# The product of w_out with phi: phi held in four column groups, the turned w_out streamed, the parts added by a second product

## The chip, the core and the metric

The kernel runs on one core of a Trainium2 chip. The metric is the device time of one execution in microseconds; the number that counts is the median of several. Before the change it is 575.36 us (three runs, 575.34 to 577.53).

## What is computed

Causal attention with a decay, then a dense feed-forward layer, then a soft mixture of experts; every result leaves in float32.

```python
x = attention(q, k, v, f)                  # 4 x 8 heads, 576 positions, head size 64 -> 2304 x 512
h = x @ w_in                               # 512 -> 2048
g = h * (1.0 / (1.0 + np.exp(-1.702 * h)))
x = g @ w_out                              # 2048 -> 512
logits = x @ phi                           # 512 -> 32 slots
d = softmax(logits, axis=0); slot_input = d.T @ x
slot_out[e] = relu(slot_input[e] @ w1[e]) @ w2[e]    # 8 experts, 4 slots each
out = softmax(logits, axis=1) @ slot_out
```

The kernel never forms the logits from `x`. It forms `wphi = w_out @ phi` (2048 x 32) once and computes the logits as `g @ wphi`. The change concerns how `wphi` is made.

## The kernel before

Attention goes through 20 rows (four batches, each with four blocks of 128 positions and one of 64). The feed-forward layer goes through nine chunks of 256 tokens, each in eight units (`moe_steps`, L765): twelve matmuls into one PSUM tile `hp` (L775 to L777), a tanh on ScalarE (L788), a product on VectorE (L789). A finished unit is later turned by `turn` (L731): four transposes (L744), a copy on ScalarE (L751), and four products with `wphi` (L753), whose stationary operand is a 128x32 slice of `wphi`, one for each of four groups of 32 output partitions. Attention work is emitted between the units, and the expert weights are loaded once attention is over, since they take its memory.

`w_out` (2048 x 512) comes in 16 slices of 128 rows. Each is loaded by SyncE's queue (L195), rebuilt as float32 from its raw words by GpSimd, ScalarE and VectorE (L208 to L216), and handed to `fold_phi` (L240). That turns the slice on TensorE (four 128x128 transposes, L243, into the PSUM tile `woT`), copies it to SBUF on ScalarE (L245), and waits for a second slice. With two slices turned, it multiplies: for each slice `n` and each quarter `kk` of the 512 columns, the turned 128x128 quarter of the slice is stationary and the 128x32 quarter of `phi_sb` moves (L252), four products adding up in PSUM to one 128x32 result. VectorE copies the two results into `wphi` (L255). There are eight such pairs. A float32 matmul shows as two instructions in the trace, so the 64 products are 128 instructions.

The 128x128 matrix `rsum` (L80, filled at L120) has a one wherever a row and a column have the same number modulo 32; a product with its first 32 columns adds four groups of 32 partitions. The kernel already uses it so in `slot_steps` (L828, and L831, which is the shape that the change uses).

The PSUM tiles `woT`, `wps`, `hp`, `gT`, `mT` and some of the slot sums share one ring of three banks (`ps_mm`, L64). The order of the instructions on each engine, and of the transfers on SyncE's queue, is made by a planner from the order of emission and from estimated costs (L1257); TensorE, ScalarE and VectorE then run their queues in that order.

Of the kernel before, what the change touches and what calls it, by code (L numbers as in the profile page):

```python
# [10 lines left out]
F32 = mybir.dt.float32  # L11
# [19 lines left out]
def attention_moe_softmoe(ctx, tc, q, k, v, f, w_in, w_out, phi, w1, w2, out):  # L31
    nc = tc.nc
# [4 lines left out]
    NS = phi.shape[1]  # L37
# [6 lines left out]
    KD = DM // 128  # L44
# [11 lines left out]
    ap_ = attn_pool.enter_context(tc.tile_pool(name="ap", bufs=1))  # L56
# [7 lines left out]
    def ps_mm(name):  # L64
        return ps.tile([128, 512], F32, tag="mm", name=name, bufs=3)
# [14 lines left out]
    rsum = const.tile([128, 4 * NS], F32, name="rsum")  # L80
    wphi = mp.tile([128, KF, NS], F32, tag="wphi", name="wphi")
    phi_sb = const.tile([128, KD, NS], F32, name="phi_sb")
# [137 lines left out]
    def more_w(to):  # L220
        while w_at[0] < min(NW, to):
            n = w_at[0]
            w_at[0] += 1
            while w_loaded[0] < min(NW, n + W_AHEAD):
                w_load(w_loaded[0])
                w_loaded[0] += 1
            w_first(n)
            if n < NI:
                split_one(n)
            else:  # L230
                WO[n - NI] = W32.pop(n)
                if w_phi:
                    fold_phi(*w_phi.pop())
                w_phi.append((n - NI,))
        if w_at[0] == NW and w_phi:
            fold_phi(*w_phi.pop())
# [3 lines left out]
    def fold_phi(ff):  # L240
        pt = ps_mm("woT")
        for kk in range(KD):
            nc.tensor.transpose(pt[:, kk * 128:(kk + 1) * 128], WO[ff][:, kk * 128:(kk + 1) * 128], ident)  # L243
        wt_ = mp.tile([128, 512], F32, tag="gt", name="woT", bufs=N_GT)
        nc.scalar.copy(out=wt_, in_=pt)  # L245
        wot.append(wt_)
        if len(wot) < 2:
            return
        wps = ps_mm("wps")[:, 0:2 * NS].rearrange("p (f s) -> p f s", s=NS)
        for n, wt_ in enumerate(wot):  # L250
            for kk in range(KD):
                nc.tensor.matmul(  # L252
                    wps[:, n], lhsT=wt_[:, kk * 128:(kk + 1) * 128], rhs=phi_sb[:, kk, :], start=(kk == 0), stop=(kk == KD - 1)
                )
        nc.vector.tensor_copy(wphi[:, ff + 1 - 2:ff + 1, :], wps)  # L255
        wot.clear()
        folded[0] = (ff + 1) // 4
# [376 lines left out]
    for pair in range(B // 2):  # L634
# [4 lines left out]
        n = rows_of[-1]  # L639
# [399 lines left out]
    if True:  # L1039
# [26 lines left out]
        n = 0  # L1066
# [10 lines left out]
        for c in range(NCH):  # L1077
            t0, t1 = goals[c], goals[c + 1]
            NSTEP = 2 * N_UNIT
            n = 0  # L1080
# [35 lines left out]
        for hf in range(2):  # L1116
            for g in range(4):
# [3 lines left out]
                    start=True, stop=True,  # L1121
# [18 lines left out]
        for hf in range(2):  # L1140
            hsb[hf] = G[NCH - 1, 1, "ab"[hf]].rearrange("p a n -> p (a n)")
            for n in range(2):
                l1 = ps_mm("l1")
                for kk in range(KD):
                    for g in range(4):
# [3 lines left out]
                            rhs=wt[1, n, e, kk], start=(kk == 0), stop=(kk == KD - 1),  # L1149
                        )  # L1150
                    load_e(4)
                if done:
                    turn(*done[-1])
                nc.scalar.activation(
                    out=hsb[hf][:, n * 512:(n + 1) * 512], in_=l1, func=AF.Relu, scale=zi[:, hf:hf + 1]
# [9 lines left out]
        for j in range(WHOLE):  # L1165
            hf, fb = divmod(j, KE)
            for p, (c0, c1) in enumerate(PARTS):
                for g in range(4):
                    nc.tensor.matmul(
                        so[p][32 * g:32 * g + 2 * SPE, :], lhsT=hz[:, fb, hf, g, :],  # L1170
                        rhs=wt[2, None, 4 * hf + g, fb][:, c0:c1], start=(j == 0), stop=False,
# [5 lines left out]
        for p, (c0, c1) in enumerate(PARTS):  # L1177
            w = c1 - c0
            nr = 2
            for fb in range(WHOLE - KE, KE):  # L1180
                for g in range(4):
                    nc.tensor.matmul(
                        so[p][32 * g:32 * g + 2 * SPE, :], lhsT=hz[:, fb, 1, g, :],
                        rhs=wt[2, p, 4 + g, fb // 2 * 2][:, fb % 2 * w:fb % 2 * w + w],
                        start=False, stop=(fb == KE - 1),
# [10 lines left out]
                out=s4[64:128], in0=p4[64:128], scalar=SS, in1=s4[64:128], op0=ALU.mult, op1=ALU.subtract  # L1196
# [13 lines left out]
            for k, blks in enumerate(groups):  # L1210
# [10 lines left out]
                if len(blk_tok[blks[0]]) == 1:  # L1221
                    tok = blk_tok[blks[0]][0][2]
                    queue.dma_start(
                        out=out[tok:tok + 128 * m, c0:c1].rearrange("(t p) n -> p t n", p=128), in_=ob
# [37 lines left out]
```

## Time and profile before

| what | value |
|---|---|
| median of three runs | 575.36 us |
| the profiled execution, its own time | 572.58 us |
| its span | 570.9 us |
| mean granted TensorE clock | 0.97 of full speed |
| PE / DVE / ACT / POOL busy | 510.8 / 353.3 / 309.6 / 69.0 us |
| stretch in which w_out is folded with phi | about 85 to 165 us |

The profile is one execution. Its time is 0.5% below the median of the runs, so a difference is worked out against 572.58 us and then carried to the median in proportion. "PE" is TensorE's matmuls, "PEld" its loads of stationary operands, which may overlap them; busy TensorE time includes a modelled tail of each instruction. The chain of waits follows the work that ended last back from the end of the execution: a piece of it is the time from one instruction to the next one on the chain, so that for instructions in a row it is their spacing and not their latency.

### The profile page before, as it was taken

To read this page: it belongs to the slowest core of one execution; us is meant where nothing else is said; L and a number is where in the kernel's file an instruction comes from. 1 tells how busy PE (TensorE), PEld (TensorE's weight loads), DVE (VectorE), ACT (ScalarE), POOL (GpSimd) and SP (SyncE) were. 2 spreads that over 40 slices of the span, in tenths; PEclk is the share of its full clock that TensorE was granted. 3 is DMA by queue.
4 is the path that set the end of the run, shared out by engine and by line. 5 is a ranking of instruction groups with operands and counts; after the bars stand their busy time and mean duration, and the time that the engine had idled before them with its cause. 6 is when DMAs were issued, how large, how long until landed. Compare 5 with 4: busy or idle time off the path is not lost.

```text
span 570.9 us, 13573 instructions
## 1 busy us (share of the span) xinstructions
PE 510.8 (89%) x5355; PEld 328.1 (57%) x5355; DVE 353.3 (62%) x934; ACT 309.6 (54%) x596; POOL 69.0 (12%) x120
## 2 busy tenths in 40 slices
PE   4476999999899989989999998988999999999991
PEld 4364877777666556655665664655566554454441
DVE  8978969476755676757685766867565323343032
ACT  5767686666765665646675565665565133312111
POOL 4766643220000000000000000000000000000000
PEclk9969799999999999999999998998999999999997
DMA  9997673978952869997648889986553189999998
GB/s 241 270 355 168 167 126 134 206 183 163 165 95 43 150 101 132 167 180 126 125 87 159 134 158 175 200 139 91 81 94 72 24 276 357 372 388 358 378 302 262
DMA packets 229823, 105.63 MB, mean 185 GB/s; under 512 B 202592, under 2 KB 211296, under 8 KB 229760
## 3 DMA queue, kind: packets, MB, share of 16 engines
q1 hardware_dynamic: 228528, 103.59, 77.9%
q10 hardware_dynamic: 1232, 1.18, 0.7%
q8 instruction: 42, 0.69, 0.5%
q14 instruction: 21, 0.17, 0.1%
HBM read 64.63 MB, written 4.72 MB: 121 GB/s over the span
## 4 chain that ended last, share of the span: by engine, by line
PE 62%; DMA 17%; DVE 9%; ACT 5%; issue 3%; SPq 2%; POOL 0%; DVEq 0%; ACTq 0%; POOLq 0%
PE hp L775 9%; PE hp L777 8%; PE hp L776 8%; DMA ph<-pn 6%; PE gT L744 5%; DMA we<-in_moe_w_dram 4%; PE p L753 4%; PE pv L607 3%; PE sp L896 3%; DMA kf<-in_k_dram 2%; PE pv L612 2%; DMA qf<-in_q_dram 2%; PE scs L536 2%; PE scs L535 2%; DVE low L213 1%
## 5 line engine op out<-in xcount | busy, mean ns | idle before, releaser
L775 PE MATMUL hp<-w,xt 128*128 128x512 f16 x288 | 111.0, 385 | 0.8 <-DVE spart L903 0.8
L776 PE MATMUL hp<-w,xt 128*128 128x512 f16 x288 | 110.7, 384 | 0.0
L777 PE MATMUL hp<-w,xt 128*128 128x512 f16 x288 | 110.6, 384 | 0.0
L562 ACT ACTIVATE pf<-scs,mx 128x512 f32<-128x512 f32 (+3 forms) x108 | 58.3, 543 | 40.7 <-DVE mx L558 30.4
L788 ACT ACTIVATE g<-hp 128x512 f32<-128x512 f32 x72 | 42.6, 592 | 53.0 <-PE hp L777 52.9
L571 DVE SCALAR_TENSOR_TENSOR pn<-pf,pn 128x512 f16<-128x512 f32 (+2 forms) x78 | 51.0, 657 | 32.1 <-ACT pn L570 31.6
L789 DVE SCALAR_TENSOR_TENSOR g<-g,hp 128x512 f32<-128x512 f32 x72 | 49.2, 683 | 34.6 <-ACT g L788 34.4
L570 ACT ACTIVATE pn<-pf 128x512 f16<-128x512 f32 (+2 forms) x78 | 46.9, 604 | 23.4 <-DMA ph<-pn 22.3
L558 DVE CUSTOM_DVE_ANT_0 scs<-scs,zmq 128x256 f32<-128x256 f32 (+3 forms) x96 | 46.9, 497 | 11.8 <-PE scs L536 6.8
L612 PE MATMUL pv<-vv,ph 128*128 128x65 f16 (+2 forms) x360 | 46.7, 198 | 3.5 <-DMA ph<-pn 3.4
L751 ACT COPY gt<-gT 128x512 f32<-128x512 f32 x71 | 40.8, 582 | 14.3 <-PE gT L744 13.5
L777 PEld LDWEIGHTS <-xt 128*128 128x128 f16 x288 | 28.5, 99 | 34.7 <-issue 2.8
L613 PE MATMUL pv<-vv,ph 128*128 128x65 f16 (+2 forms) x360 | 46.1, 196 | 0.0
L614 PE MATMUL pv<-vv,ph 128*128 128x65 f16 (+2 forms) x360 | 45.4, 194 | 0.0
L744 PE MATMUL gT<-ident,g 128*128 128x128 f32 x288 | 44.5, 278 | 1.0 <-DVE g L789 1.0
L775 PEld LDWEIGHTS <-xt 128*128 128x128 f16 x288 | 29.0, 101 | 25.7 <-issue 3.5
L612 PEld LDWEIGHTS <-ph 128*128 128x128 f16 (+2 forms) x360 | 34.5, 101 | 14.6 <-issue 5.8
L776 PEld LDWEIGHTS <-xt 128*128 128x128 f16 x288 | 28.5, 99 | 24.0 <-issue 2.3
L744 PEld LDWEIGHTS gT<-ident,g 128*128 128x128 f32 x288 | 33.3, 142 | 14.2 <-issue 5.1
L535 PE MATMUL scs<-kab,qa 128*128 128x128 f16 x240 | 35.4, 219 | 4.4 <-ACT pf L562 2.5
L613 PEld LDWEIGHTS <-ph 128*128 128x128 f16 (+2 forms) x360 | 34.9, 103 | 2.7 <-issue 0.4
L614 PEld LDWEIGHTS <-ph 128*128 128x128 f16 (+2 forms) x360 | 35.0, 103 | 0.7 <-issue 0.6
(223 smaller groups left out, 1013.4 us busy)
## 6 DMA issues: line engine op xcount, KB each, us to landing
we<-in_moe_w_dram SPq DMA_DIRECT2D x127, 256.0 KB, 5.4
raw<-in_moe_w_in_dram SPq DMA_DIRECT2D x16, 512.0 KB, 7.6
raw<-in_moe_w_out_dram SPq DMA_DIRECT2D x16, 512.0 KB, 6.0
kf<-in_k_dram SPq DMA_DIRECT2D x13, 256.0 KB, 3.7
qf<-in_q_dram SPq DMA_DIRECT2D x13, 256.0 KB, 4.4
vf<-in_v_dram SPq DMA_DIRECT2D x12, 256.0 KB, 4.5
out_dram<-ob SPq DMA_DIRECT2D x12, 256.0 KB, 3.2
ph<-pn SPq DMA_TRANSPOSE x78, 3.3
```

The source lines that it names most:

```text
L558: nc.vector.tensor_tensor_reduce(out=o, in0=o, in1=mask, scale=-SC, scalar=3.0e38 if n == 128 else DG[r][1][:, u], op0=ALU.add, op1=ALU.mi ...
L562: nc.scalar.activation(out=pf[:, hh * nb:(hh + 1) * nb], in_=o, func=AF.Exp, bias=mx[:, hh:hh + 1], scale=-1.0)
L570: nc.scalar.activation(out=pn[:, 0, 0:w], in_=pf, func=AF.Copy, scale=PB)
L571: nc.vector.scalar_tensor_tensor(out=pn[:, 1, 0:w], in0=pf, scalar=PB, in1=pn[:, 0, 0:w], op0=ALU.mult, op1=ALU.subtract)
L612: nc.tensor.matmul(o, lhsT=ph[0:rr, 0, off:off + n], rhs=vh, start=(j == 0), stop=False)
L613: nc.tensor.matmul(o, lhsT=ph[0:rr, 0, off:off + n], rhs=vl, start=False, stop=False)
L614: nc.tensor.matmul(o, lhsT=ph[0:rr, 1, off:off + n], rhs=vh, start=False, stop=(j == i))
L744: last_turn[0] = nc.tensor.transpose((pt if a < 2 else pt2)[:, a * 128:(a + 1) * 128], g[:, a * 128:(a + 1) * 128], ident)
L775: nc.tensor.matmul(hp, lhsT=xt[:, 0, kk, ts], rhs=win(0, fg, kk), start=(kk == 0), stop=False)
L776: nc.tensor.matmul(hp, lhsT=xt[:, 0, kk, ts], rhs=win(1, fg, kk), start=False, stop=False)
L777: last_hp[0] = nc.tensor.matmul(hp, lhsT=xt[:, 1, kk, ts], rhs=win(0, fg, kk), start=False, stop=(kk == KD - 1))
L789: nc.vector.scalar_tensor_tensor(out=g, in0=g, scalar=1.0, in1=hp, op0=ALU.add, op1=ALU.mult)
```

## The change

Inside `fold_phi`, the operands of the product change places. The 128x32 quarter of `phi_sb` is now stationary and the turned 128x128 quarter of `w_out` moves; the quarter `kk` writes to output partitions 32·kk to 32·kk + 31 of a new PSUM tile `wq`. The four quarters are no longer added in PSUM. ScalarE copies the 128x256 tile to SBUF (`part`), and two products, with a 128x128 half of `part` stationary and `rsum[:, 0:32]` moving, add the quarters and give the same 128x64 result `wps`, which VectorE copies into `wphi` as before.

```diff
-        wps = ps_mm("wps")[:, 0:2 * NS].rearrange("p (f s) -> p f s", s=NS)
+        wq = ps_mm("wq")[:, 0:256]
         for n, wt_ in enumerate(wot):
             for kk in range(KD):
                 nc.tensor.matmul(
-                    wps[:, n], lhsT=wt_[:, kk * 128:(kk + 1) * 128], rhs=phi_sb[:, kk, :], start=(kk == 0), stop=(kk == KD - 1)
-                )
+                    wq[NS * kk:NS * (kk + 1), n * 128:(n + 1) * 128], lhsT=phi_sb[:, kk, :],
+                    rhs=wt_[:, kk * 128:(kk + 1) * 128], start=True, stop=True,
+                )
+        part = ap_.tile([128, 256], F32, tag="part", name="part")
+        nc.scalar.copy(out=part, in_=wq)
+        wps = ps_mm("wps")[:, 0:2 * NS].rearrange("p (f s) -> p f s", s=NS)
+        for n in range(2):
+            nc.tensor.matmul(
+                wps[:, n], lhsT=part[:, n * 128:(n + 1) * 128], rhs=rsum[:, 0:NS], start=True, stop=True
+            )
         nc.vector.tensor_copy(wphi[:, ff + 1 - 2:ff + 1, :], wps)
```

## Rows read from the trace of the kernel before

**Rows 1.** Windows: start:end, length; busy us (instructions) by engine; clock; DMA share; GB/s.
```profile
90.00:105.00 15.00, 15.00 (x192) 13.03 (x192) 13.06 (x28) 11.31 (x21) 5.75 (x7) 1.00 0.46 85
135.00:150.00 15.00, 13.33 (x123) 9.78 (x123) 10.88 (x39) 11.84 (x26) 0.00 (x0) 1.00 1.04 199
150.00:165.00 15.00, 13.36 (x160) 10.76 (x158) 9.47 (x27) 9.61 (x19) 0.00 (x0) 1.00 0.85 132
345.00:360.00 15.00, 13.44 (x141) 7.41 (x142) 10.22 (x39) 8.15 (x19) 0.46 (x8) 0.89 0.93 173
```

**Rows 2.** Chain of waits, 84 to 165 us: start, us, what; the matmuls of L252.
```profile
91.71 0.37 PE wps L252 x4
...
93.91 0.81 PE wps L252 x8
...
128.31 1.01 PE wps L252 x8
...
157.96 0.89 PE wps L252 x8
```

**Rows 3.** The same chain, its longest pieces that are not TensorE's.
```profile
105.39 6.11 DMA raw<-in_moe_w_out_dram
137.48 4.88 DMA kf<-in_k_dram
152.31 5.22 DMA ph<-pn
160.69 2.75 DMA ph<-pn
```

**Rows 4.** The same chain: the first and the last of nine ScalarE pieces.
```profile
111.58 0.43 ACT low L211
...
163.52 0.53 ACT pn L570
```

**Rows 5.** Waits of TensorE, 85 to 167 us: who, for whom, total us, times, longest.
```profile
PE scs L535 <- ACT pf L562: 1.6, 1, 1.6
PE gT L744 <- DVE g L789: 1.0, 1, 1.0
PE wps L252 <- ACT woT L245: 0.8, 1, 0.8
PE p L753 <- ACT gt L751: 0.7, 1, 0.7
PE pv L612 <- DMA ph<-pn: 0.2, 1, 0.2
```

**Rows 6.** Chain of waits elsewhere: L753 in column groups, and what follows it.
```profile
176.70 0.79 PE p L753 x24
177.49 0.16 PE scs L535
177.65 0.06 PE scs L536
...
484.50 0.57 PE p L753 x16
...
487.37 0.22 PE hp L775
...
489.96 0.44 PE gT L744 x4
490.40 0.36 PE p L753 x8
490.76 0.32 PE hp L775
...
493.45 0.36 PE p L753 x8
493.81 0.59 PE gT L744 x4
```

**Rows 7.** Chain of waits: the product of L831 with rsum's first 32 columns.
```profile
172.36 0.36 PE lg L831 x4
```

**Rows 8.** Groups by form: line engine op, shapes, count | busy us, mean ns | idle before.
```profile
L252 PE MATMUL wps<-phi_sb,woT 128*128 128x32 f32 x128 | 16.6, 272 | 0.8 <-ACT woT L245 0.8
L747 ACT COPY gt<-gT 128x256 f32<-128x256 f32 x1 | 0.4, 372 | 2.4 <-PE gT L744 2.4
L562 ACT ACTIVATE pf<-scs,mx 128x256 f32<-128x256 f32 x24 | 11.2, 473 | 6.6 <-DVE mx L558 6.3
L570 ACT ACTIVATE pn<-pf 128x512 f16<-128x512 f32 x42 | 26.3, 629 | 12.5 <-DMA ph<-pn 11.8
```

**Rows 9.** Timeline, 502 to 508 us: start, us, engine, line; one hop over ScalarE.
```profile
504.81 0.66 PE L744 MATMUL gT<-ident,g 128*128 128x128 f32 x4
505.33 0.37 ACT L747 COPY gt<-gT 128x256 f32<-128x256 f32 x1 [2.36 <-PE gT L744]
505.82 0.72 PE L753 MATMUL p<-gt,wphi 128*32 128x128 f32 x8
```

**Rows 10.** Timeline, 155 to 170 us, TensorE and VectorE: the last pair.
```profile
161.68 0.97 PE L252 MATMUL wps<-phi_sb,woT 128*128 128x32 f32 x8
165.17 0.22 DVE L255 COPY wphi<-wps 128x64 f32<-128x64 f32 x1
166.61 0.43 PE L753 MATMUL p<-gt,wphi 128*32 128x128 f32 x8
```

## The prediction

> **What bounds the kernel now.** I read the busy time in stretches first, to see who is full where `w_out` is folded with `phi`. From 90 to 105 us TensorE is busy for the whole stretch; from 135 to 165 us it is busy for 13.3 of each 15 us, while ScalarE has 9.6 to 11.8 us of work and the transfers are dense [rows 1]. So TensorE is nearly full, but not everywhere. Next come TensorE's own waits: in the 82 us from 85 to 167 they add up to 4.3 us, of which one of 0.8 us is L252 waiting for the copy L245 [rows 5]. Last comes the chain of waits. From 84 to 165 us it runs along TensorE and leaves it for four long transfers, of 6.1, 4.9, 5.2 and 2.8 us [rows 3]. The reader should see the two together: while the chain is on a transfer, TensorE is busy with other work that is just in time, so work removed from TensorE there turns into waiting, and work removed where the chain is on TensorE shortens the kernel.
>
> L252 lies on that chain in ten pieces (four stand in the rows), 64 instructions and 6.94 us in all [rows 2]. That is half of its 128 instructions [rows 8]. Eight instructions take 6.94 / 8 = 0.87 us, so L252 costs TensorE 16 x 0.87 = 13.9 us and the chain 6.94 us.
>
> **What the change removes and adds on TensorE.** Removed: 13.9 us. Added, first: per pair 16 instructions with a 128x32 float32 stationary operand and 128 float32 columns moving, in four groups of output partitions. The trace has this form: it is L753. Eight in a row take 0.36 us, 16 take 0.57, 24 take 0.79 [rows 6]. So one more costs (0.79 - 0.36) / 16 = 0.027 us, against 0.109 for one of L252, and a group has a fixed part of 0.36 - 8 x 0.027 = 0.14 us. There is a second fixed part behind it: the first `hp` matmul after a group takes 0.32 us (a next one is 0.22), the first `scs` 0.16 instead of 0.06, four transposes 0.59 (0.44 where they follow other work) [rows 6]. I charge 0.12 us. A group of eight then costs 0.48 us and one of 16 costs 0.69. Which it will be is the planner's choice. Today the half for the first slice runs while the second slice is still being copied, and L252 stands on the chain in eights [rows 2]; I expect eights. Sixteen groups of eight are 7.7 us, eight groups of sixteen 5.5 us.
>
> The fixed part is where the Trainium skill speaks against the change. In "TensorEngine Tiling (Array Packing)", section Key Properties, it says that changing the tiling mode drains TensorE, and in its section Theoretical Speedup that a dimension of up to 32 can give a factor of up to four. The trace agrees with both, 0.109 to 0.027 inside a group and about 0.26 us for entering and leaving one; by the factor of four alone the 13.9 us would become 3.5.
>
> Added, second: the two products with `rsum` per pair, four instructions. L831 is the same shape, and four of it take 0.36 us [rows 7]; with a little for their neighbours, 8 x 0.38 = 3.0 us. TensorE therefore saves 13.9 - 7.7 - 3.0 = 3.2 us with groups of eight and 13.9 - 5.5 - 3.0 = 5.4 us with groups of sixteen. On the chain lie half of the pieces: 1.6 to 2.7 us. I take the middle, 2.15 us.
>
> **What it adds elsewhere.** ScalarE gets eight copies of 128x256 float32 from PSUM. The trace has one such copy, 372 ns, and an exponential of the same size at 473 ns [rows 8]: 3.0 to 3.8 us of work, in 80 us where ScalarE is busy two thirds of the time. ScalarE holds nine pieces, 4.75 us, of the 81 us of chain, 6% [rows 4]; so 0.2 us of the copies lie on the path, and at worst all 3.8. The copy stands in ScalarE's queue ahead of exponentials and of `pn` (L570), and those are followed by the transposing transfers for attention.
>
> The new wait is on TensorE: the product with `rsum` waits for the copy, and everything queued on TensorE behind it waits too. The nearest rows are the 16 hops from L243 over L245 to L252, of which one cost TensorE 0.8 us [rows 5]. Half as many hops of that kind cost 0.4 us; a copy that is not covered costs more (below). I take 0.6 us and keep 0 and 9.6 as the ends.
>
> Nothing else moves: the loads of `w_out`, the transposes L243, the copies L245 and L255 stay as many. A pair holds a bank of the ring of three twice instead of once. No wait of TensorE in this stretch is for a bank as far as the rows show, so I cost it at nothing; the cover is the planner's freedom to put attention ahead of an `hp`, and if it is gone, the price is that of another hop. `wphi` is ready later by a copy and a product, about 0.8 us. For the last pair the matmuls start at 161.68, L255 runs at 165.17 and the first product after it at 166.61 us [rows 10]; the copy of L255 stands in VectorE's queue longer than the added steps take, so that is hidden.
>
> **Sum.** -2.15 + 0.2 + 0.6 = -1.35 us, taken as -1.4. Against the profiled execution, 572.58 us, that is 571.2; in proportion, 575.36 x 571.2 / 572.58 = 574.0 us. All later stages, the expert weights too, follow from the end of attention, so I let the shift stand to the end.
>
> **The rivals.** A measurement of this kernel can tell about 0.5% (2.9 us) from no change.
>
> 1. TensorE is the limit all along: the transfers on the chain are released by work that itself waited for TensorE, so that all 3.2 to 5.4 us arrive. For it speak the few waits of TensorE, 4.3 us in 82 [rows 5]; against it the 13.3 of 15 us between 135 and 165 [rows 1] and the four long transfers [rows 3]. About -4.2 us: 571.1 us, between 570 and 572.
>
> 2. Slower, by the uncovered hop: TensorE runs in order and stands still at each pair until ScalarE has delivered `part`. One uncovered hop shows at the end of the kernel: transposes from 504.81, four of them 0.44 us, the copy at 505.33, the next product at 505.82 [rows 9], so 505.82 - 505.25 = 0.57 us. With one instruction ahead on ScalarE, 0.63 us for L570 [rows 8], it is 1.2 us, and eight hops cost 9.6. TensorE then stands still in full, so its whole saving counts: -3.2 to -5.4 + 9.6 = +4 to +6, about 580 us. It decides from the wait per pair: 3.2 / 8 = 0.4 us eats the saving, and 0.76 us makes the kernel slower by 0.5%. Against it speaks that 15 of 16 hops of today are covered.
>
> 3. The planner sorts the queues anew, as the costs of the operations differ, and a transposing transfer or a load goes out behind its neighbour instead of ahead of it. A piece of the chain of this kind is 2.8 to 5.2 us [rows 3], so this is worth 3 to 5 us either way: 570 or 578 us. A stretch in which TensorE then idles can also lose clock: in 345 to 360 us the mean granted clock is 0.89 [rows 1], which is 22% of the 15 us, 3.3 us, at the lower level of 1.2 GHz and so some 1.6 us of work.
>
> **How the numbers follow.** The forecast has 0.46, rival 1 0.24, rival 2 0.14, rival 3 0.16 (0.06 faster, 0.04 same, 0.06 slower). The forecast reaches from -3.2 to +1 and gives 0.04 to faster and 0.42 to same; rival 1 is faster. Faster: 0.04 + 0.24 + 0.06 = 0.34. Same: 0.42 + 0.04 = 0.46. Slower: 0.14 + 0.06 = 0.20. The range runs from just below rival 1, 569.2 us, to the dearer end of rival 3 with a lost stretch of clock, 578.8 us; it leaves out most of rival 2 and the ends of rival 3.
>
> **What would show it.** The new matmuls of the product in groups of eight at about 0.36 us apiece on the chain, or sixteen at 0.57; the products with `rsum` at 0.36 us for four; eight copies of about 0.37 us on ScalarE; TensorE's busy time lower by 3 to 6 us; few waits of TensorE for `part`. The forecast is wrong if TensorE waits for ScalarE's copy at most of the pairs, if the saved time is still there at 165 us and gone at 450, or if a span of the same length shows other transfers on the chain than before.

## The result, and the profile after

The kernel with the change takes 568.77 us (median of six runs, 566.11 to 570.59) against 575.35 us for the kernel before on the same chip: a ratio of 0.9865 with a 95% interval of 0.9828 to 0.9903. The forecast was 574.0 us in a range from 569.2 to 578.8; the result lies just below it. The two medians are 6.6 us apart; by the ratio, which is used below throughout, the gain is 7.8 us (1.35% of 575.35), and by its interval 5.6 to 9.9. The forecast's 1.4 us is a quarter of the lowest of these. The profiled execution of after took 569.88 us with a span of 568.1 us. Executions more than 1.5% above the fastest of their kernel (the slow ones) are left out of all that follows, which leaves 94 of the 103 runs of before that were timed beside the experiments, and a ratio is turned into us with their median, 574.0 us.

Behind L263 the lines of after are 8 higher than those of before; the column products keep L252, the copy of the part is L257, the products with `rsum` are L260.

The windows of after that answer to [rows 1] (start:end, length; busy us and instructions of PE, PEld, DVE, ACT, POOL; clock; DMA share; GB/s):

```profile
90.00:105.00 15.00, 15.00 (x201) 11.78 (x204) 14.53 (x30) 12.33 (x23) 7.07 (x8) 1.00 0.58 124
135.00:150.00 15.00, 10.31 (x145) 6.98 (x142) 9.90 (x31) 9.23 (x19) 0.00 (x0) 1.00 1.12 174
150.00:165.00 15.00, 13.43 (x148) 9.39 (x148) 7.70 (x23) 8.58 (x18) 0.00 (x0) 0.77 0.40 74
345.00:360.00 15.00, 15.00 (x169) 8.90 (x167) 11.02 (x43) 7.89 (x20) 0.61 (x8) 1.00 0.93 170
```

In the stretch of the fold, TensorE is idle more than before (10.3 busy of 15 us instead of 13.3) and has lost clock behind it (0.77). At 345 us, where the edit touches nothing, TensorE is now full and has its whole clock, where before showed 13.4 us and 0.89. The last copy into `wphi` (L263) starts later than before's 165.17 us [rows 10]:

```profile
L263 DVE COPY wphi<-wps x8: 208/216/221, 96.4 to 170.8; 128x64 f32<-128x64 f32 x8
```

The gain is not where the edit is.

The chain of waits of after, 84 to 165 us (start, us, what; answers to [rows 2, 3, 7]):

```profile
93.28 0.36 PE wq L252 x8
...
94.57 0.56 PE wps L260 x4
...
101.29 5.24 DMA kf<-in_k_dram
...
108.34 0.45 PE wps L260 x4
...
120.11 0.63 PE wps L260 x4
...
134.82 4.99 DMA kab<-kan
...
145.19 5.01 DMA ph<-pn
...
150.22 0.52 ACT pn L578
150.75 0.27 ACT part L257
151.06 1.06 PE wps L260 x4
```

Eight column products take 0.36 us, as worked out from L753. The products with `rsum` take 0.45 to 0.63 us and not 0.36, and the one at 151.06 us takes 1.06, at a lower clock. The four lines from 145.19 us on are the hop of rival 2 in a form that the prediction did not see: the copy of the part stands on ScalarE behind a `pn`, and that waits for a transposing transfer.

TensorE's waits of after, 85 to 167 us (who, for whom, us in total, times, longest; answers to [rows 5]):

```profile
PE wps L260 <- ACT part L257: 5.5, 3, 4.6
PE scs L459 <- ACT pf L481: 1.5, 1, 1.5
PE p L761 <- ACT gt L759: 0.8, 1, 0.8
PE pv L620 <- DVE x L634: 0.3, 1, 0.3
```

and the windows around the longest of them (columns as above):

```profile
147.00:150.00 3.00, 0.00 (x0) 0.00 (x0) 2.12 (x7) 1.63 (x3) 0.00 (x0) 1.00 1.33 135
150.00:153.00 3.00, 1.94 (x9) 1.85 (x10) 2.72 (x8) 2.31 (x5) 0.00 (x0) 0.60 0.95 163
153.00:156.00 3.00, 3.00 (x9) 1.06 (x7) 0.64 (x2) 1.07 (x2) 0.00 (x0) 0.50 0.38 70
156.00:159.00 3.00, 3.00 (x27) 1.85 (x25) 0.42 (x1) 0.88 (x2) 0.00 (x0) 0.76 0.00 0
```

TensorE stands still for 4.6 us, and then works for some 7 us at the lower level of 1.2 GHz. All waits of the stretch add up to 8.1 us, against 4.3 before. So after is faster in spite of a worse fold, 5.6 us later at its end (3.8 us in the repeats: 166.8 against 163.0).

### The profile page after: what moved, and what is told of

Its sections match the earlier page's. It is cut to its first block, busy times and chain, and to the rows that moved or that the text cites. A ratio compares the mean times of both kernels' runs of the same rounds, so it can differ in the third digit from the quotient of the medians.

```text
span 568.1 us, 13632 instructions
## 1 busy us (share of the span) xinstructions
PE 508.9 (90%) x5387; PEld 319.4 (56%) x5387; DVE 352.7 (62%) x934; ACT 309.8 (55%) x604; POOL 69.4 (12%) x120
## 4 chain that ended last, share of the span: by engine, by line
PE 66%; DMA 16%; DVE 7%; ACT 5%; issue 2%; SPq 1%; POOL 0%; DVEq 0%; ACTq 0%; POOLq 0%
PE hp L783 10%; PE hp L784 9%; PE hp L785 9%; DMA ph<-pn 7%; PE gT L752 5%; DMA we<-in_moe_w_dram 5%; PE p L761 4%; PE pv L615 3%; PE sp L904 3%; PE pv L620 3%; DMA kf<-in_k_dram 2%; PE scs L543 2%; PE pv L622 2%; PE scs L544 2%; PE pv L621 2%
## 5 line engine op out<-in xcount | busy, mean ns | idle before, releaser
L752 PE MATMUL gT<-ident,g 128*128 128x128 f32 x288 | 46.1, 280 | 0.0
L620 PEld LDWEIGHTS <-ph 128*128 128x128 f16 (+2 forms) x360 | 34.2, 101 | 18.4 <-issue 10.3
L752 PEld LDWEIGHTS gT<-ident,g 128*128 128x128 f32 x288 | 33.2, 142 | 13.4 <-issue 5.7
L577 POOL MEMSET pn<- 128x128 f16 x12 | 2.5, 211 | 268.3 <-DMA ph<-pn 113.9
```

Source lines behind the costliest of these rows:

```text
L620: nc.tensor.matmul(o, lhsT=ph[0:rr, 0, off:off + n], rhs=vh, start=(j == 0), stop=False)
L752: last_turn[0] = nc.tensor.transpose((pt if a < 2 else pt2)[:, a * 128:(a + 1) * 128], g[:, a * 128:(a + 1) * 128], ident)
```

## The experiments

**The floor and the repeat.** The unchanged kernel before, and the change once more.

> The kernel before, once more, as a control: ratio 1.000 within 0.3%. Its second profile shows which of the first one's stalls and clock losses belong to the kernel (they stand at the same place) and which to one execution. The first profiled execution was 572.58 us and the timed ones about 575.35; if the 2.8 us between them are chance of one execution, this profile lies between 572 and 577 us with the same order of work on each engine.

576.4 us, a ratio of 1.0055 (1.0023 to 1.0086) for the very same program, outside the 0.3% that were expected. Differences of half a per cent are not to be read, whatever their interval.

> The changed kernel once more, beside the others of this group. As in its first comparison: 0.9865 of the kernel before. The kernel before against itself had come out at 1.0055 in the last group, so 0.982 to 0.992 would agree.

566.18 us, 0.9858 (0.9812 to 0.9903). The gain repeats.

**The terms of the sum.** First the part copied by VectorE, so that it no longer stands behind `pn`:

```diff
-        nc.scalar.copy(out=part, in_=wq)
+        nc.vector.tensor_copy(part, wq)
```

> The changed kernel with the copy of part on VectorE instead of ScalarE; all TensorE work is the same. Theory A (the kernel shortens by the TensorE time that the change saves): 568 to 570 us as the changed kernel, since TensorE has the same work; the 13 us for which TensorE waited for part move to VectorE or shrink. Theory B (the gain is the planner's new order of the queues, and another order gives another time): no relation to 568.8; anything from 566 to 577 us.

564.32 us, 0.986 (0.9826 to 0.9894). TensorE's waits of this run, 75 to 175 us, show the hop nearly gone:

```profile
PE wps L260 <- DVE part L257: 1.7, 2, 1.2
```

The 13 us of the expectation count the waits of TensorE's products (6.0 us) and of their loads (7.2 us), which are largely the same. The ratio is that of the change within its interval. The long hop costs less than these runs can tell.

Then the column products issued twice:

```diff
-                nc.tensor.matmul(
-                    wq[NS * kk:NS * (kk + 1), n * 128:(n + 1) * 128], lhsT=phi_sb[:, kk, :], ...
+                for _ in range(2):
+                    nc.tensor.matmul(
+                        wq[NS * kk:NS * (kk + 1), n * 128:(n + 1) * 128], lhsT=phi_sb[:, kk, :], ...
```

> The changed kernel with each product in the column groups issued twice (the second writes the same values): 128 more instructions, at 0.027 us apiece 3.4 us more TensorE time, and no other change. Theory A: 568.8 + 3.4 = 572.2 us. The prediction's rule, half of it: 570.5. Theory B: a new order again, anything from 566 to 577 us.

575.71 us, 1.0049 (1.0016 to 1.0082). 128 more instructions at 0.027 us are 3.5 us, and the kernel is 10.6 us slower than the change (1.0049 less 0.9865, of 574.0). Two thirds of that are not the work that was added.

And the product of before cut to one of its four quarters:

```diff
-            for kk in range(KD):
+            for kk in range(1):
```

> The kernel before with only the first of the four products of each sum (wphi is then a quarter of the sum): 96 of 128 instructions of 0.109 us leave TensorE, 10.4 us, with no new hop and no new copy. Theory A: 565 us (all 10.4 us arrive). The prediction's own rule, half of it lies on the chain: 570 us. Theory B: no clear relation to the TensorE time taken away; it may be no faster than 572.

554.8 us, 0.9691 (0.9657 to 0.9725), or 17.7 us, where three quarters of L252's 13.9 us, 10.4 us of TensorE's time, were taken out. Again the time moved by more than the work. In each of these kernels the planner had sorted the queues anew. In the traces the queues can be compared instruction by instruction. Of TensorE's 5227 instructions outside the fold's own products, 373 in e2 and 1242 in e4 stand in another order than in the change, and 1173 in e3 in another than in before.

**Work and order apart.** The order of every engine's queue was recorded from before and from after, and then forced on other work by an edge (an added dependency) from each instruction to the next:

```diff
+        for text in ORDER:
+            keys = [int(x) for x in text.split()]
+            for x, y in zip(keys, keys[1:]):
+                tc.add_manual_dep(by[y], by[x].name, ..., reason="order")
```

> The product as in the kernel before (the old operands, no part, no products with rsum), but every engine's queue in the order of the changed kernel, as recorded from its program; SyncE's queue is the same instruction by instruction. Theory A (the TensorE time saved is the gain): as the kernel before, ratio 1.00. Theory B (the new order is the gain): as the changed kernel, 0.986 to 0.99.

567.23 us, 0.9878 (0.9836 to 0.9919): the product of before in the order of after has nearly all of the gain, 7.0 us, without the change. Its trace holds the queues of after on every engine, but for the fold's own products and copies.

> The product as in the changed kernel (wps in a free part of wq's bank), but every engine's queue in the order of the kernel before; only the eight copies of part and the sixteen products with rsum are put in by the planner, and L255 is free. Theory A: as the changed kernel, 0.986 to 0.99; by my prediction's sum 0.9975; if all 3.2 to 5.4 us arrive 0.991 to 0.994. Theory B: 1.00, or above it by the hops.

571.93 us, 0.9953 (0.9919 to 0.9988): the product of after in the order of before gains 2.7 us, no more than before differed from itself in e1. Here `wps` had to share the bank of `wq`, which brings one wait of 2.5 us of its own (the waits view of this run: `wq` for VectorE's `wphi`), so that the work alone may be worth up to 5 us in the old order; in the new order it is worth 0.7 us (0.9878 less 0.9865, inside the noise).

> Only the first of the four products of each sum, as in e3 (wphi is a quarter of the sum), with every engine's queue in the order of the kernel before. It takes 10.4 us off TensorE and changes nothing else. Theory A: -10.4 us, ratio 0.982, or half of it by the rule of the chain, 0.991. Theory B, in which most of e3's 18.5 us came from the new order: 0.99 to 1.00. If it comes out near e3's 0.969, neither the order nor the plain TensorE time explains it.

564.15 us, 0.9826 (0.978 to 0.9873). In the old order, 10.0 us are gained for some 10.4 us taken off TensorE. Half of them, 5.2 us, lies outside the interval (7.3 to 12.6), and the other 7.7 us of the free quarter came from its order. That the 10.0 us are TensorE's work alone is not shown: the three stalls that the next part finds in before are gone too (no wait of TensorE between 170 and 370 us is over 1.1 us), and the mean clock is 0.967 against 0.9625.

No run forced the old order on the old work alone. But the queues of this run, and of e9, e13 and e14 below, are in the traces those of before on every engine, but for what was left out or filled in. So the edges themselves changed no order.

**What a good order has.** TensorE's waits between 170 and 370 us, of the repeat of before and then of the old work in the new order:

```profile
PE pv L612 <- DMA ph<-pn: 3.1, 1, 3.1
PE lg L828 <- DVE l L820: 2.3, 1, 2.3
PE scs L535 <- DMA qa<-qan: 1.8, 1, 1.8
```

```profile
PE p L980 <- ACT gt L978: 2.3, 4, 1.2
PE pv L839 <- DMA ph<-pn: 1.1, 2, 0.8
PE pv L839 <- DVE x L853: 1.0, 1, 1.0
```

The old work in the old order has three single stalls of 1.8 to 3.1 us, which the first profile of before shows as well (2.8, 2.3 and 1.9 us, at 207, 251 and 346.5 us); the new order has none above 1.2 there. The stalls belong to work and order together: with the new work in the old order (e7) TensorE has no wait over 1.4 us between 170 and 370 us, though that profile is of the fastest of its 12 executions. The windows behind the stalls, of the repeat of before, and then the same windows of the new order (columns as above):

```profile
204.00:207.00 3.00, 1.67 (x21) 1.48 (x21) 1.74 (x7) 1.98 (x6) 0.00 (x0) 0.50 0.47 89
207.00:210.00 3.00, 3.00 (x10) 1.27 (x10) 2.87 (x12) 1.35 (x3) 0.00 (x0) 0.50 0.00 0
...
252.00:255.00 3.00, 3.00 (x10) 2.10 (x11) 2.06 (x7) 0.20 (x1) 0.18 (x2) 0.50 0.92 176
255.00:258.00 3.00, 3.00 (x14) 1.51 (x12) 1.53 (x8) 0.45 (x3) 0.00 (x0) 0.50 1.11 242
...
351.00:354.00 3.00, 3.00 (x44) 2.66 (x44) 1.78 (x9) 1.38 (x4) 0.00 (x0) 0.50 0.95 180
```

```profile
207.00:210.00 3.00, 3.00 (x24) 1.38 (x24) 2.90 (x11) 1.08 (x4) 0.00 (x0) 1.00 1.23 111
...
252.00:255.00 3.00, 3.00 (x30) 0.96 (x28) 2.92 (x11) 2.63 (x6) 0.00 (x0) 1.00 1.12 195
255.00:258.00 3.00, 3.00 (x35) 1.80 (x28) 3.00 (x9) 2.25 (x5) 0.00 (x0) 1.00 1.04 150
```

The reader should see TensorE busy for 3.00 of 3.00 us in both, but with 10 instructions at clock 0.50 and 24 at 1.00. Busy time alone hides the loss. The same two places in the first profile of before, behind stalls of 2.8 and 2.3 us, have their whole clock:

```profile
207.00:210.00 3.00, 3.00 (x31) 1.87 (x32) 2.65 (x11) 2.53 (x6) 0.00 (x0) 1.00 0.46 87
252.00:255.00 3.00, 3.00 (x21) 1.68 (x21) 2.74 (x13) 0.74 (x4) 0.18 (x2) 1.00 0.95 195
```

That led to a theory, the theory A of the next expectations (further up the letter stood for the work): the order gains clock. A run of TensorE at 1.2 GHz follows a stall, in some executions of the old order and not in others.

To test it, products whose results the next product overwrites were put where TensorE stands still, in the old work and the old order:

```diff
+FILL = {2241: 60, 2758: 16, 4230: 24}   # ahead of which instruction, how many products
...
+            for _ in range(FILL[n]):
+                nc.tensor.matmul(out_, lhsT=ident16[:, 0:rows], rhs=rhs, start=True, stop=True)
```

> The product of before, every queue held to the order recorded from before, and in three places where TensorE stands still in every execution of that order (2.8 to 3.1 us ahead of L612 near 207 us, 2.3 us ahead of L828 near 251 us, 1.9 us ahead of L535 near 346 us) products whose results the next product overwrites: 60 of 65 columns, 16 of 256 and 24 of 128, so that TensorE is busy while it waits. Theory A (most of the 6.8 us that the new order is worth is clock that the old order loses after these stalls): the mean granted clock of the timed runs rises from 0.9615 to 0.968 to 0.973, no fall stands near 204 to 210, 252 to 258 and 350 to 357 us, and the ratio to before is 0.988 to 0.995. Rival B (the order is worth its time through who waits for whom, and the clock follows it): the ratio is 0.999 to 1.006, since the added products are at best hidden. Rival C (the falls move to the next stall): clock as before, 0.9615, ratio 0.998 to 1.005.

570.41 us, 0.9952 (0.9918 to 0.9985), mean clock 0.9717: the clock is as theory A has it, the time a hair beyond its dear end. One fall is still there, against the theory. TensorE's timeline around 250 us (start, us, engine, line, what; idle before it) and a window behind it show why:

```profile
250.49 3.57 PE L297 MATMUL lg<-ident 128*128 128x256 f16 x16 [2.67 <-DVE l L1063]
```

```profile
252.00:255.00 3.00, 3.00 (x15) 2.28 (x13) 0.00 (x0) 0.00 (x0) 0.00 (x0) 0.50 0.98 200
```

The filling at the second place waited itself, 2.67 us for VectorE's `l`, and then ran for 3.57 us at half clock. The next run puts it ahead of the last group before the stall.

> As e9_filled_stalls (the product and the order of before, overwritten products where TensorE stands still), but at the second place they stand ahead of the last scores-times-values group before the stall instead of behind the wait for VectorE's l, where they had waited too and then ran for 3.6 us at half clock. 70 products of 65 columns near 207 us, 60 of 65 columns near 248 us, 24 of 128 columns near 346 us. Theory A (the old order loses clock after its stalls, and that is what the new order gains): mean granted clock of the timed runs 0.972 to 0.977 and a ratio of 0.985 to 0.992, since the 3.4 us that the misplaced products cost are gone. Rival B (the gain of e9_filled_stalls is a shift of the order's timing, not clock): a ratio of 0.994 to 1.003 and a clock as in e9_filled_stalls or lower.

566.69 us, 0.9898 (0.9843 to 0.9952), mean clock 0.9732. Timeline and windows of this run:

```profile
203.15 2.29 PE L297 MATMUL pv<-ident 128*128 128x65 f16 x70
...
206.35 0.20 PE L855 MATMUL pv<-vv,ph 128*128 128x65 f16 x1 [0.91 <-DMA ph<-pn]
...
247.44 2.09 PE L297 MATMUL pv<-ident 128*64 128x65 f16 x60
```

```profile
207.00:210.00 3.00, 3.00 (x20) 1.54 (x18) 2.56 (x11) 1.86 (x4) 0.00 (x0) 1.00 0.34 64
252.00:255.00 3.00, 3.00 (x26) 2.05 (x25) 2.38 (x14) 1.81 (x6) 0.00 (x0) 1.00 1.09 213
```

2.3, 2.1 and 1.5 us of useless work, 5.9 us in all, make the kernel of before 5.9 us faster and give it the clock of the new order. The data for which TensorE waited come no sooner for it: ahead of 206.35 us, 2.29 us of filling and 0.91 of waiting are 3.2 us, where the stall had 2.8 and 3.1.

> The control: as many overwritten products, 33, 30 and 24 of 128 columns, some 5 us in all, in the same order of before, but each placed some us behind a stall, where TensorE is busy anyway. Theory A: they fill nothing, so the mean granted clock stays at 0.959 to 0.964 and the ratio is 1.004 to 1.010. Rival B (more activity anywhere, or a shift of timing, helps): clock 0.967 or more, ratio below 1.000.

571.31 us, 0.9965 (0.9933 to 0.9996), clock 0.9692. This went against what theory A expected of it, and clock and ratio are both those of rival B: as much added work, where TensorE is busy, neither slowed the kernel nor left the clock alone. The trace shows that the control was not a clean one:

```profile
205.45 0.20 PE L855 MATMUL pv<-vv,ph 128*128 128x65 f16 x1 [2.84 <-DMA ph<-pn]
216.78 2.01 PE L297 MATMUL scs<-ident 128*128 128x128 f16 x33
```

```profile
207.00:210.00 3.00, 3.00 (x9) 1.12 (x8) 2.44 (x12) 1.35 (x3) 0.00 (x0) 0.54 0.24 49
249.00:252.00 3.00, 3.00 (x37) 2.44 (x37) 2.05 (x6) 1.22 (x2) 0.50 (x10) 1.00 0.86 169
252.00:255.00 3.00, 3.00 (x21) 1.69 (x20) 2.32 (x13) 1.20 (x5) 0.14 (x2) 1.00 0.93 179
348.00:351.00 3.00, 2.90 (x54) 2.33 (x47) 2.79 (x14) 2.18 (x6) 0.00 (x0) 0.78 0.94 179
```

The first stall has its 2.84 us and its fall, as in before. But TensorE comes to the second place some 2 us later than it would have, the data are there, and that stall is gone: added work upstream may do as well as work in the stall. At the third place, too, the 1.8 us have become two waits of 0.58 and 0.41 us, and yet the clock falls behind them (0.78). So e14 does not tell filling from shifting, and a fall does not need one long stall. It does show that 5.3 us of added work (2.0, 1.8 and 1.5 us) can cost nothing.

**Are new orders good ones?** Two edits that add and remove no work. Here the second slice of a pair goes first:

```diff
-        for n, wt_ in enumerate(wot):
+        for n, wt_ in reversed(list(enumerate(wot))):
```

> The product of before, with the same 128 instructions of L252, emitted for the second slice of a pair ahead of the first; nothing else is edited and the planner sorts the queues from it anew. No work is added or removed. Theory (the planner's new order decides by several us whatever the edit is): a ratio outside 0.995 to 1.005, either sign, most likely 0.985 to 0.993 or 1.007 to 1.015; clock and time move together. Rival (new orders scatter little, and the gain of the order of after is special to its work): 0.997 to 1.003.

567.45 us, 0.9888 (0.9849 to 0.9926): 6.4 us for an edit that does no work. Of TensorE's 5227 instructions outside the fold's products, 1209 stand in another order than in before.

Here the first slice is multiplied as soon as it is turned:

```diff
+        if n == 0:
+            w_ps.append(ps_mm("wps")[:, 0:2 * NS].rearrange("p (f s) -> p f s", s=NS))
+        wot.append(wt_)
+        wps = w_ps[-1]
+        for kk in range(KD):
+            nc.tensor.matmul(wps[:, n], lhsT=wt_[:, kk * 128:(kk + 1) * 128], rhs=phi_sb[:, kk, :], ...)
+        if len(wot) < 2:
+            return
```

> The product of before, with the same 128 instructions of L252, but those of the first slice of a pair are emitted as soon as that slice is turned, and its bank of the ring is taken there; nothing else is edited, and the planner sorts the queues anew. No work is added or removed. Theory (the planner's order decides): a ratio outside 0.995 to 1.005, either sign. Rival (orders scatter little): 0.997 to 1.003. If this and the run with the second slice first both stay within 0.5% of before, the order of after is a rare find; if one is faster by over 1%, the 6.8 us can be had without any change of work.

577.19 us, 1.006 (1.0025 to 1.0095), which can't be told from the 1.0055 of before itself. The same two edits on the kernel after:

> The change, with the column products of the second slice of a pair emitted ahead of those of the first; no work is added or removed, and the planner sorts the queues anew. It answers e10_second_slice_first, which is the same edit of the kernel before. Theory (work of the change 2 to 3 us, the rest is which order the planner happens to make): a ratio to before anywhere from 0.980 to 1.002, and not the same as that of the change, 0.9865, by more than 0.3%. Rival (the operations of the change lead the planner to a good order, whatever the emission): 0.984 to 0.988.

565.43 us, 0.9857 (0.9811 to 0.9902): no other than the change, as the rival has it. But it is hardly another order: 57 of the 5227 instructions stand otherwise than in the change. What does differ is the hop, 0.5 us in all between 75 and 175 us instead of 6.0, and that brought nothing that can be told.

> The change, with the column products of the first slice of a pair emitted as soon as it is turned, and its bank taken there; the same edit as e11_first_slice_early, on the change. Theory: 0.980 to 1.002, as that edit was worth +0.6% on the kernel before and the work of the change is worth 0.4%: most likely near 1.000. Rival (the operations lead to a good order): 0.984 to 0.988.

585.35 us, 1.021 (1.0165 to 1.0255): the operations of the change, in a kernel 3.5% slower than the change. It is slower than either theory has it. The edit also holds a bank of the ring for longer, so it is not an order alone. Windows of this run:

```profile
125.00:150.00 25.00, 19.00 (x168) 11.98 (x168) 16.99 (x50) 14.84 (x31) 1.26 (x7) 0.80 1.05 181
150.00:175.00 25.00, 20.54 (x218) 13.75 (x219) 14.17 (x42) 13.41 (x28) 0.00 (x0) 0.84 0.72 115
```

TensorE has both idle time and lost clock there; its mean clock over the timed runs is 0.953, the lowest of all.

**Without the hop, as it was meant.** The products with `rsum` are emitted at the next fold, with the part copied on VectorE:

```diff
+        finish_phi()                       # products with rsum and copy to wphi of the pair before
         pt = ps_mm("woT")
...
+        nc.vector.tensor_copy(part, wq)
+        late_w.append((part, ff))
```

> The change, with the part copied on VectorE and its two products with rsum emitted at the next fold, ahead of that slice's transposes, so that TensorE has other work while the part is copied. Planner free. Theory: no wait of TensorE for the part over 0.3 us (the change has four, 6.0 us in all), no clock fall near 150 to 158 us; against the change that is worth up to 2 us, so a ratio to before of 0.978 to 0.987 if the planner's new order is as good as that of the change, and up to 0.995 if it is as that of before. Rival (the hop is covered anyway by transfers that are late): as the run with the part on VectorE, 0.984 to 0.988.

564.67 us, 0.9842 (0.9797 to 0.9887). The waits view still has 1.7 us for the part, the longest 1.2, against the 0.3 of the expectation. These are the waits of e2, and the traces say why: e12 and e2 hold the same instructions in the same order on every engine. The edit did not reach the queues, so that e12 measures e2 (0.986) once more. The same with the copy left on ScalarE:

> As e12_sum_one_fold_later, but the part is copied on ScalarE as in the change. No wait of TensorE for the part over 0.5 us. Theory: 0.980 to 1.000 by the order that comes out; rival (the operations lead to a good order): 0.984 to 0.988.

567.36 us, 0.9887 (0.9844 to 0.9931). Here TensorE waits 5.9 us for the part, 4.6 of it once, as in the change, and the queues are those of the change, instruction by instruction: e17 is a third measurement of it. And e12 with the second slice first:

> e12_sum_one_fold_later with the second slice's column products emitted first. A draw of another order for the best work so far. Theory: 0.975 to 1.000; it beats the change only if the order is as good as that of e12_sum_one_fold_later. Rival (the operations lead to a good order): 0.982 to 0.986.

570.08 us, 0.994 (0.9914 to 0.9966). This one has an order of its own (1106 of the 5227 instructions stand otherwise than in the change), and it is slower than e2 with the same operations, by 0.8 to 1%. So no kernel was made in which later products cover the hop.

The runs side by side. "Clock missing" is the mean time of the timed runs, times one less their mean granted clock:

| kernel | ratio to before | us | mean clock | clock missing, us |
|---|---|---|---|---|
| before, 94 runs | 1 | 0 | 0.9625 | 21.5 |
| old work, new order (e6) | 0.9878 | -7.0 | 0.9735 | 15.0 |
| old work, old order, stalls filled (e13) | 0.9898 | -5.9 | 0.973 | 15.2 |
| old work, second slice first (e10) | 0.9888 | -6.4 | 0.966 | 19.1 |
| old work, first slice early (e11) | 1.006 | +3.4 | 0.964 | 20.7 |
| new work, old order (e7) | 0.9953 | -2.7 | 0.966 | 19.3 |
| the change | 0.9865 | -7.7 | 0.971 | 16.5 |
| the change, part on VectorE (e12, as e2) | 0.9842 | -9.1 | 0.9735 | 15.0 |
| the change, first slice early (e16) | 1.021 | +12.1 | 0.953 | 27.3 |

## Why the prediction was wrong

**The step that failed: the sum has no term for the planner's new order.** The prediction named it as rival 3, priced it at 3 to 5 us of either sign, and gave it 0.16; the sum itself says "Nothing else moves" and lets the shift stand to the end. It is the largest term: -7.0 us with the work unchanged (e6), against 2.7 for the work in the old order (e7). It was no small chance either, as nearly every free edit made the planner sort anew. The kernels with orders of their own (the change, e2, e10, e11, e16 and e18) stand between 0.986 and 1.021, and e10, whose work is that of before, moved by over four times the forecast. With such a term the range had to reach over 1% to either side, and the chances of no change had to be small. The prediction's remark that lost clock belongs to this rival [rows 1] was the right thread: the 0.89 at 345 us was the trace of a stall (1.9 us, at 346.5) that the new order has not.

**The term for the work agrees with the runs as far as they can tell, and by luck.** The sum gave -1.35 us; alone in the old order the work brought -2.7 (-4.7 to -0.7), hardly clear of the half per cent of e1. It comes out by two errors that cancel. From the start of each L252 to TensorE's next instruction, before adds up to 14.1 us and its repeat to 14.9, with one group at half clock; the sum had 13.9. After has 5.9 us for the column products in 20 groups, and with 0.12 us behind each 8.3; the sum had 7.7 for 16. The products with `rsum` take 4.1 us, 0.51 per pair (0.45 to 0.47 seven times, and 0.87 at half clock), where the sum had 0.38 from the one price of L831: that term was too small. TensorE so saves 1.7 to 2.5 us, not 3.2 to 5.4; the sum then let half of that arrive, where the runs do not show a half (below).

**What held.** The column products go in eights for the most part (14 of the 20 groups), at 0.36 us, the eight copies on ScalarE take 373 ns each, as the one copy of the rows did, and other transfers stand on the chain than before, which the prediction named as a sign that it is wrong. TensorE's busy time fell from 510.8 to 508.9 us only, less than the 3 to 6 us that were to be seen; it contains the stretch at half clock.

**"Half of it lies on the chain" did not hold either.** The quarter in the old order gave 10.0 us for some 10.4 us of TensorE, if with more clock than before. This fits rival 1: the chain leaves TensorE for long transfers [rows 3], and those would be released by work that TensorE had done before. No run followed such a transfer back, so that the mechanism stays argued. The chain of waits showed which work ended last; it couldn't show whether less work on TensorE would move the transfers too. Rival 1 had a saving twice too large.

**The hop of rival 2 came, and its price did not.** TensorE waited 5.5 us for the part in the stretch, 4.6 of it once, for a reason that the prediction had in hand (the copy in ScalarE's queue, ahead of `pn`) but turned the wrong way round: the copy stood behind a `pn` that waited for a transfer. Taking most of that wait away (e2, e12, e15) gave nothing that can be told from the change. Where its 4.6 us are made up for is open.

**How the order gains.** Shown: the order alone is worth 7.0 us; the old work in the old order has three stalls between 170 and 370 us after which TensorE runs at 1.2 GHz in part of its executions; the new order has neither the stalls nor the falls there; useless work in the stalls gives the old order the new one's clock and, within the intervals, its time. The change, e2, e6 and their like (e5, e12, e15, e17, whose queues are theirs or nearly so), and e13, miss 15.0 to 16.5 us of clock where before misses 21.5; but for e13 that is one family of orders, and no count of independent cases. Not shown: that clock is all of it. Among the 94 runs of before, 0.01 of clock goes with 2.3 us of time, where 5.7 would be the whole, so by this estimate the 6.5 us of clock that e6 got back may be worth anything from 2.6 to 6.5 of its 7.0 us. And e10 gains 6.4 us with 2.4 us of clock: most of that must come otherwise, and through which waits stays open. Nor do all falls follow such stalls: in the first profile of before TensorE, with 1.57 us busy in 393 to 396 us but no single wait over 0.8, has 0.58 in the next 3 us. The two first profiles have about the same clock (0.970 before, 0.972 after), so that the mean over the timed runs carries this argument. Why the planner's sorting for the new operations was good stays open too; e16 and e18 have the same operations, and theirs were not.

The Trainium skill describes the like in "TensorE: Matmul & The Clock Gate", section "HAM oscillation — how this bites in real kernels": waits for transfers between pieces of work send TensorE back to the slower clock. The windows of this case agree where TensorE waited 3.1 us for a transfer (0.50 behind it). Here 0.50 stands also behind a wait of 2.3 us for VectorE, and in another execution the clock was whole behind 2.8 us.

## What to carry to other kernels

Where a planner sorts the queues, an edit is two changes: its work and a new order, and the second may be the larger; pin the recorded order on both versions before a gain is put down to the work, and let the range of a forecast hold what an edit without work does. Compare the queues of two kernels in their traces before an experiment is read: here two edits had left them as they were. Look at the granted clock and the number of instructions of a window beside its busy time: a full window at 0.5 is half empty. A chain of waits that runs through transfers does not show that time taken off the busy engine is lost there: in e8 nearly all of it arrived, though the clock rose with it.

## What was not expected of the hardware

- A stall of 2 to 3 us can cost more than itself: after it TensorE ran at 1.2 GHz for some 3 to 7 us in the executions where the clock fell (0.50 from 252 to 258 us in the repeat of before; 0.61 and then 0.82 from 348 to 354 us in its first profile; behind the 4.6 us of after, 0.60, 0.50 and 0.76 from 150 to 159 us). The same stall in another execution of the same program had no fall: 2.8 us ahead of 207 us in the first profile of before.
- 5.9 us of useless products made a kernel 5.9 us faster (e13), and 5.3 us of them placed elsewhere did not make it slower (e14).
- Eight instructions with 32 output partitions each, in four groups, take 0.36 us both as L753 and as L252; four of the product with `rsum` took 0.36 us in one place [rows 7] and 0.45 to 0.63 in others.
